# Turning the attended heads on VectorE in an adaLN transformer block on one core

## The chip, the cores and the metric

The kernel runs on one core of one Trainium2 chip. A core has TensorE (matmuls into PSUM), VectorE, ScalarE (ACT), GpSimd (POOL), SyncE (SP, which here only issues DMAs and waits), 16 DMA engines, SBUF with 128 partitions, and PSUM, which the kernel uses as eight buffers of 128 x 512 f32. The metric is the device time of one execution in microseconds (us).

## The reference

One transformer block with adaptive layer norm, batch 1, 2048 rows, width 640, 32 heads of 20 channels, feed-forward width 1536, everything in bfloat16:

```
mod = (silu(c) @ w_mod) -> sa, ca, ga, sb, cb, gb        (six rows of 640)
h = layernorm(x) * (1 + ca) + sa
q, k, v = split(h @ wqkv)                                 (32 heads of 20)
s = q k^T / sqrt(20), kept where 0 <= i - j < 256, else -1e9
x = x + ga * (concat_heads(softmax(s) v) @ wo)
h = layernorm(x) * (1 + cb) + sb
x = x + gb * ((sigmoid(h @ w_gate) * (h @ w_up)) @ w_down)
```

## The kernel before, in words

The 2048 rows are worked in eight chunks of 256 (two blocks of 128 rows). Of each chunk: the layer norm's statistics (VectorE, L781) and a normalized copy `x0`; a turn to channels-on-partitions `hT` (TensorE for chunks 0 and 1, transposing DMAs on SyncE from chunk 2, L810); modulate on VectorE, ACT or POOL (L827, L828); Q, K, V by `wq`, `wk`, `wv` (`qkv`, 5 matmuls of 128x128 by 320 each). Q and K leave PSUM through casts into a staging tile `stg`, each head in 32 columns, and are turned into `QT`, `KT` (TensorE for chunks 0 and 1, DMAs on SyncE after). Scores of one half chunk (16 heads, `q` = 0 or 1) are made transposed, keys on partitions, four heads at a time in row groups of TensorE; ACT takes the exp out of PSUM (L1054, L1028, L1091), POOL masks the window's edges (L1059, L1063, L1032), and `burst` multiplies by V, which carries columns of ones, so that the sums of the softmax come out beside the heads. In chunks from 1 on, the PV matmuls of one half chunk stand in one TensorE block with the scores of the next (`with_pv`).

The attended chunk then stands with 32 channel rows per head (20, and a row of the sum) on partitions and rows of x along the free axis. `norm` turns it in blocks of 32 x 32 on VectorE (`tr1`, L1150, twice per half chunk), takes reciprocals (L1155), multiplies (divide, L1157) into `Tn`, and turns back (`tr2`, L1159) into `On`. `close` writes the 20 used rows of each of four row groups to DRAM (four DMAs on SyncE to `doc`, helper L576), and reads them back into `oT` as channels packed on 128 partitions (one DMA per half chunk). `outproj` multiplies `oT` by `wo`, adds x (L1240), and goes on with the second norm, its turn (`h2T`, DMAs on SyncE, L810) and `mlp`: gate and up by pairs of 128-channel tiles, tanh on ACT (L1285), the product on VectorE (L1287), and `wd`, with the residual add (L1306) and the store. The output of attention and of the MLP is scaled by the gates `ga`, `gb`: instead, `wo` (`wos`, L1331) and `wd` (`wds`, L1268) are multiplied once by the broadcast gate `gbc`, which takes a small trip through DRAM (`gate`, then `gbc`, both on SyncE).

The order of every instruction on every engine is fixed beforehand: the program lists some 2000 operations, and `PLAN` is a permutation of them with an engine for each (`schedule`, L151). The planner follows the list with a model of durations only to hand out buffers; `emit` (L262) writes each engine's stream in that order, with waits on semaphores. So an operation that waits holds up everything behind it in its engine's stream, DMA issues on SyncE included. TensorE's two kinds of blocks, whole-array matmuls (helper line L686) and matmuls in row or column groups (L687: scores, PV, the modulation), alternate in the order given.

Of the kernel before, what the change touches and what calls it, by code (L numbers as in the profile page):

```python
# [8 lines left out]
ALU = mybir.AluOpType  # L9
# [4 lines left out]
D = 640  # L14
H = 32
DH = 20
# [332 lines left out]
def c_pe(n):  # L349
# [118 lines left out]
]  # L468
TR1 = 2
NPH = 2  # L470
NPQ = 2
PQ = ()
# [26 lines left out]
def build(nc, A_x, A_wqkv, A_wo, B_x, B_w_gate, B_w_up, B_w_down, c, w_mod, out, S=2048):  # L499
# [59 lines left out]
    def R(name):  # L559
        return Res(name)  # L560
# [825 lines left out]
```

## Time and profile before

| | us |
|---|---|
| median of 3 runs | 326.38 (326.34 to 329.38) |
| profiled execution | 326.74 |
| its span | 324.8 |
| TensorE busy | 316.1 (97%) |
| ScalarE busy | 213.0 (66%) |
| VectorE busy | 205.6 (63%) |
| GpSimd busy | 188.0 (58%) |
| TensorE idle, 11.3 to 80 us | 2.89 |
| TensorE idle, 80 to 322.2 us | 0.02 |

How to read the rows shown below. A timeline row has the start, the time from the start of the first to the end of the last instruction of the row, the engine and line, the operation, `out<-in`, the shapes and the count, and in brackets the idle time ahead with the engine and line that ended it. "issue" is a wait for nothing that the profile shows. PE is TensorE's matmuls, PEld its weight loads, SPq SyncE's issuing of DMAs. A row of groups has the count, then busy us, mean ns of one, and idle time ahead with its releasers. Matmuls are pipelined and their ends are modelled; starts are what to compare.

### The profile page before, as it was taken

The page shows a single profiled execution, that of the slowest core. Times are in us where ns is not written, and L with a number is a line of the kernel's source. Part 1 is how long each engine was busy: PE and PEld are TensorE (multiplying, and loading weights), DVE is VectorE, ACT ScalarE, POOL GpSimd, SP SyncE. Part 2 cuts the span into 40 slices and gives each one's busy share as a digit, 9 for nine tenths or more (in the row PEclk, how much of TensorE's full clock was granted, in tenths as well). Part 3 has the DMA queues.
Part 4 walks back from the last instruction along what each step waited for, and adds up shares of the span by engine and source line. Part 5 has one row for each costly group of instructions (what it writes and reads, how often), then busy time and mean ns, then how long its engine had stood idle before and what let it go on. Part 6 is the DMA issues. An engine that isn't in the chain of part 4 may idle for free.

```text
span 324.8 us, 11997 instructions
## 1 busy us (share of the span) xinstructions
PE 316.1 (97%) x5044; PEld 236.8 (73%) x5045; DVE 205.6 (63%) x426; ACT 213.0 (66%) x228; POOL 188.0 (58%) x349
## 2 busy tenths in 40 slices
PE   6999999989999999999999999999999999999996
PEld 2666767667776777776787777777888777887885
DVE  4699987768686865674755647464845376645423
ACT  2699984788678877988685857676886756320220
POOL 5337858855868677948774846676583958001000
PEclk9999999999999999999999999999999999999999
DMA  7999989998648464726551303465121206112201
GB/s 238 370 315 245 281 161 189 207 192 281 186 91 140 64 139 75 109 60 130 118 71 26 83 2 73 126 65 120 39 47 28 77 22 83 38 46 41 83 0 42
DMA packets 73023, 38.20 MB, mean 118 GB/s; under 512 B 46602, under 2 KB 71690, under 8 KB 72970
## 3 DMA queue, kind: packets, MB, share of 16 engines
q1 hardware_dynamic: 71808, 36.13, 50.6%
q10 hardware_dynamic: 1162, 1.31, 1.5%
q8 instruction: 40, 0.66, 0.9%
q14 instruction: 13, 0.11, 0.1%
HBM read 21.30 MB, written 5.25 MB: 82 GB/s over the span
## 4 chain that ended last, share of the span: by engine, by line
PE 76%; DVE 0%; issue 0%
PE M L686 64%; PE S L687 6%; PE M L687 5%; DVE x L1306 0%
## 5 line engine op out<-in xcount | busy, mean ns | idle before, releaser
L1054 ACT ACTIVATE E<-S 128x2048 bf16<-128x2048 f32 x56 | 105.0, 1876 | 45.7 <-PE S L687 45.4
L1063 POOL TENSOR_SCALAR_AFFINE_SELECT E<-E 128x512 bf16<-128x512 bf16 x112 | 69.6, 635 | 8.4 <-DVE Tn L1157 2.1
L1059 POOL TENSOR_SCALAR_AFFINE_SELECT E<-E 128x256 bf16<-128x256 bf16 x112 | 45.4, 415 | 48.3 <-PE M L686 14.8
L686 PE MATMUL M<-h2T,wu 128*128 128x256 bf16 x480 | 68.0, 273 | 0.5 <-DVE h2T L828 0.5
L686 PE MATMUL M<-h2T,wg 128*128 128x256 bf16 x480 | 67.0, 273 | 0.0
L686 PE MATMUL M<-wd,hh 128*128 128x320 bf16 (+2 forms) x396 | 57.3, 296 | 0.0
L1287 DVE SCALAR_TENSOR_TENSOR hh<-sig,M 128x512 bf16<-128x512 f32 x48 | 32.2, 680 | 34.9 <-ACT sig L1285 24.1
L686 PEld LDWEIGHTS M<-h2T,wu 128*128 128x128 bf16 x480 | 45.3, 98 | 8.4 <-issue 0.7
L686 PEld LDWEIGHTS M<-h2T,wg 128*128 128x128 bf16 x480 | 45.5, 98 | 6.9 <-DVE T L1150 0.2
L686 PEld LDWEIGHTS M<-wd,hh 128*128 128x128 bf16 x396 | 37.0, 98 | 14.0 <-DVE hh L1287 0.2
L1285 ACT ACTIVATE sig<-M 128x512 f32<-128x512 f32 x48 | 28.2, 596 | 27.7 <-PE M L686 27.1
L1032 POOL TENSOR_SCALAR_AFFINE_SELECT E<-E 128x1024 bf16<-128x1024 bf16 x28 | 31.9, 1144 | 6.8 <-DVE st L781 2.5
L1306 DVE TENSOR_TENSOR x<-M,x 128x320 bf16<-128x320 f32 (+2 forms) x33 | 15.7, 479 | 29.4 <-PE M L686 28.9
L687 PE MATMUL S<-QT,KT 20*64 20x256 bf16 (+5 forms) x1856 | 32.3, 228 | 1.3 <-issue 0.7
L687 PEld LDWEIGHTS S<-QT,KT 20*64 20x64 bf16 (+1 forms) x1856 | 20.0, 100 | 18.4 <-issue 8.8
L781 DVE BATCH_NORM_STATS2 st<-x 128x6 f32<-128x320 bf16 x64 | 28.9, 477 | 1.3 <-DMA x<-in_A_x_dram 1.0
L1150 DVE STREAM_TRANSPOSE T<-M 128x512 f32<-128x512 f32 x32 | 21.4, 698 | 13.1 <-PE S L687 10.5
L1028 ACT ACTIVATE E<-S 128x2048 bf16<-128x2048 f32 x14 | 26.3, 1876 | 5.1 <-PE S L687 5.0
L686 PE MATMUL M<-wq,hT 128*128 128x320 bf16 x160 | 25.9, 300 | 1.5 <-ACT hT L827 0.9
L686 PE MATMUL M<-wv,hT 128*128 128x320 bf16 x160 | 26.8, 300 | 0.0
L686 PE MATMUL M<-wk,hT 128*128 128x320 bf16 x160 | 26.2, 300 | 0.0
L686 PE MATMUL M<-wo,oT 128*128 128x320 bf16 x160 | 24.8, 300 | 0.0
(86 smaller groups left out, 362.7 us busy)
## 6 DMA issues: line engine op xcount, KB each, us to landing
x<-in_A_x_dram SPq DMA_DIRECT2D x19, 160.0 KB, 8.4
doc<-On SPq DMA_DIRECT2D x64, 40.0 KB
out_dram<-x SPq DMA_DIRECT2D x14, 160.0 KB, 1.8
wd<-in_w_mod_dram SPq DMA_DIRECT2D x6, 320.0 KB
wd<-in_B_w_down_dram SPq DMA_DIRECT2D x4, 480.0 KB
wu<-in_w_mod_dram SPq DMA_DIRECT2D x5, 320.0 KB
oT<-doc SPq DMA_DIRECT2D x8, 192.0 KB
wg<-in_B_w_gate_dram SPq DMA_DIRECT2D x2, 576.0 KB
```

What stands on the lines that cost most here:

```text
L686: return e.matmul(o, l, r, start=st, stop=sp, skip_group_check=True)
L687: return e.matmul(o, l, r, start=st, stop=sp, tile_position=tp, skip_group_check=True)
L781: A("dve", lambda e, g, bi=bi, j=j: e.bn_stats(v(bi * 12 + j * 6, 6), src[bi].ap[:, j * 320:(j + 1) * 320]), 0.48, reads=[src[bi].r()], wr ...
L1028: A("act", lambda e, eng: e.activation(cell().rearrange("p m (x c) -> p m x c", c=64)[:, :, 0:4:3, :], Sp.ap[:].rearrange("p j (k x c) -> ...
L1032: A("pool", lambda e, eng, c0=c0, pat=pat, base=base, cm=cm: e.affine_select(cell()[:, :, c0:c0 + 64], cell()[:, :, c0:c0 + 64], pattern=p ...
L1054: A("act", lambda e, eng: e.activation(part(0, 512), Sp.ap[:], ACT.Exp, scale=SM_SCALE), 1.876, reads=[Sp.r()], writes=[E.r("C"), E.r("B") ...
L1059: A("pool", lambda e, eng, hc=hc, src=src, far_h=far_h: e.affine_select(side(hc), part(src, 64), pattern=[[0, 4], [-1 if far_h else 1, 64] ...
L1063: A("pool", lambda e, eng, c0=c0, near=near: e.affine_select(part(c0, 128), part(c0, 128), pattern=[[0, 4], [1 if near else -1, 128]], com ...
L1150: A("dve", lambda e, g, h=h: e.transpose(T1.ap[:, 512 * h:512 * h + 512], X[h].ap), 0.694, reads=[X[h].r()], writes=[T1.r(h)], prio=3.5, t ...
L1285: A("act", lambda e, g, pg=pg, sg=sg: e.activation(sg.ap[:], pg.ap[:], ACT.Tanh, scale=0.5), c_act(512), reads=[pg.r()], writes=[sg.r()], ...
L1287: A("dve", lambda e, g, pu=pu, sg=sg, f0=f0: e.scalar_tensor_tensor(out=hh.ap[:, f0:f0 + 2, :], in0=sg.ap[:].rearrange("p (a b) -> p a b", ...
L1306: A("dve", lambda e, g, ps=ps, bi=bi, c0=c0, n=n: e.tensor_tensor(x1[bi].ap[:, c0:c0 + n], ps.ap[:, 0:n], x1[bi].ap[:, c0:c0 + n], op=ALU. ...
```

## The change

`norm` now divides into a `Tn` of 128 x 1280 that takes both half chunks, ordered so that, after the second half, two turns on VectorE (128 x 640, one per block of 128 rows) write `oT` directly. The tile `On`, the DRAM tensor `doc`, its 64 writes and 16 reads are gone, and with them the clearing of `Tn`. Each block of `oT` is waited for by itself (`oT.r(bi)`), no longer each half of the heads.

For this, heads are numbered `16q + 4j + k` (row group `j`, set `k`) instead of `4(4q + k) + j`; the cast of Q and K into `stg` permutes accordingly. Partition `32j + r` of tile `t` of `oT` now holds channel `32t + r` of the 160 channels of the eight heads of row group `j`, so `wo` is loaded with its rows in that order: sixteen DMAs of 16 partitions by 2 or 3 rows on SyncE, in place of one of 128 partitions by 5 rows. The five `wos` follow, each with its own resource.

`PLAN` is another order, with other engines for some of the casts, modulates and stores. Operations by queue or engine, before and after: SyncE 205 and 133, ACT 236 and 244, VectorE 426 and 424, POOL 337 and 337, TensorE 959 and 959. Two durations in the planner's model differ (0.29 to 0.25 and 0.25 to 0.262). All five `wos` stand on VectorE, in a row.

```diff
-TR1 = 2
...
-    p_Tn = sbpool("Tn", 1, [128, 1024])
-    p_On = sbpool("On", 1, [128, 1024])
+    p_Tn = sbpool("Tn", 1, [128, 1280])
...
+    R_wo = [R(f"wo{t}") for t in range(NDT)]
+    R_wop = {(j, x, q): R(f"wo{j}{x}{q}") for j in range(4) for x in range(2) for q in range(2)}
...
-    for i in range(len(p_Tn.aps)):
-        p_Tn.init[i].append(A("pool", lambda e, g, i=i: e.memset(p_Tn.aps[i][:], 0.0), 1.0, writes=[R("ti")], prio=3))
...
-    dma(lambda: wo[:], lambda: A_wo.rearrange("(t p) f -> p t f", p=128), 2.15, writes=[R_wo], prio=0.5, tag="wo")
+    for j in range(4):
+        for x in range(2):
+            cut = 3 - x
+            for q, t0, t1 in ((0, 0, cut), (1, cut, NDT)):
+                r0 = 80 * j + 16 * x if q == 0 else 320 + 80 * j + 16 * (1 - x)
+                dma(lambda j=j, x=x, t0=t0, t1=t1: wo[32 * j + 16 * x:32 * j + 16 * x + 16, t0:t1, :],
+                    lambda t0=t0, t1=t1, r0=r0: A_wo.rearrange("(u e) f -> e u f", e=16)[:, r0 // 16:r0 // 16 + 2 * (t1 - t0) - 1:2],
+                    0.055 * (t1 - t0), writes=[R_wop[j, x, q]], prio=0.5, tag="wo")
...
-                        h = 4 * (4 * q + k) + j
+                        h = 16 * q + 4 * j + k
...
-    def norm(X, On, a):
-        T1, Tn, Dr = Tile(p_T1, "T1"), Tile(p_Tn, "Tn"), Tile(p_Dr, "Dr")
+    def norm(X, Tn, q, a):
+        T1, Dr = Tile(p_T1, "T1"), Tile(p_Dr, "Dr")
...
-        A("dve", lambda e, g: e.tensor_tensor(blk(Tn), blk(T1), Dr.ap[:].unsqueeze(2).to_broadcast([128, 32, DH]), op=ALU.mult),
-          0.82, port=True, reads=[T1.r(0), T1.r(1), Dr.r()], writes=[Tn.r()], prio=4, tag=f"divide_{a}")
-        A("dve", lambda e, g: e.transpose(On.ap[:], Tn.ap[:]), 1.22, reads=[Tn.r()], writes=[On.r()], prio=4, tag=f"tr2_{a}")
+        A("dve", lambda e, g: e.tensor_tensor(
+            Tn.ap[:].rearrange("p (b k d) -> p k b d", k=8, d=DH)[:, 4 * q:4 * q + 4],
+            T1.ap[:].rearrange("p (k b r) -> p k b r", k=4, r=32)[:, :, :, 0:DH],
+            Dr.ap[:].rearrange("p (k b) -> p k b", k=4).unsqueeze(3).to_broadcast([128, 4, 8, DH]), op=ALU.mult),
+          0.82, port=True, reads=[T1.r(0), T1.r(1), Dr.r()], writes=[Tn.r(q)], prio=4, tag=f"divide_{a}")
...
         def close(q, X):
-            On = Tile(p_On, f"On{a}_{q}")
-            norm(X, On, a)
-            for j in range(4):
-                Rj = R(f"doc{a}_{q}_{j}")
-                dma(lambda j=j, q=q: rdoc[j * DH:(j + 1) * DH, 4 * q:4 * q + 4, :],
-                    lambda j=j, On=On: On.ap[32 * j:32 * j + DH, :].rearrange("p (g c) -> p g c", g=4), 0.22,
-                    reads=[On.r()], writes=[Rj], prio=1, tag=f"n_ow_{a}", dur=0.42)
-                R_doc[q].append(Rj)
-            t0, t1 = ((0, 2), (2, 5))[q]
-            dma(lambda t0=t0, t1=t1: oT.ap[:, t0:t1, :], lambda t0=t0, t1=t1: doc.rearrange("(t p) c -> p t c", p=128)[:, t0:t1, :],
-                0.41, reads=R_doc[0] + (R_doc[1] if q else []), writes=[oT.r(q)], prio=1.5, tag=f"oT_{a}", dur=0.5, dlat=2.88)
+            norm(X, Tn, q, a)
             if q == 1:
+                for bi in range(2):
+                    A("dve", lambda e, g, bi=bi: e.transpose(
+                        oT.ap[:, :, bi * 128:bi * 128 + 128].rearrange("p t (b c) -> p b t c", c=32), Tn.ap[:, 640 * bi:640 * bi + 640]),
+                      0.83, reads=[Tn.r(0), Tn.r(1)], writes=[oT.r(bi)], prio=4, tag=f"tr2_{a}")
                 x1, h2 = outproj(a, oT)
...
-                pe_chain(ps, 320, pairs, [[oT.r(0 if t < 2 else 1), R_wo] for t in range(NDT)], 15, f"wo{a}",
+                pe_chain(ps, 320, pairs, [[oT.r(bi), R_wo[t]] for t in range(NDT)], 15, f"wo{a}",
...
     for t in range(NDT):
         A(WSE[0], lambda e, g, t=t: e.tensor_tensor(wo[:, t, :], wo[:, t, :], gbc[:], op=ALU.mult), WS, port=True,
-          reads=[R_wo, R_gbc], writes=[R_wo], prio=20, tag="wos")
+          reads=[R_wop[j, x, int(t >= 3 - x)] for j in range(4) for x in range(2)] + [R_gbc], writes=[R_wo[t]], prio=20, tag="wos")
```

More of the change, by code (lines that the diff above doesn't have):

```diff
@@ L562, in build @@
     R_w3 = {k: [R(k + "0"), R(k + "1")] for k in ("wq", "wk", "wv")}
-    R_crow, R_ident, R_ccol, R_cth, R_siluc, R_silubc, R_wo = (R(n) for n in ("crow", "ident", "ccol", "cth", "siluc", "silubc", "wo"))
+    R_crow, R_ident, R_ccol, R_cth, R_siluc, R_silubc = (R(n) for n in ("crow", "ident", "ccol", "cth", "siluc", "silubc"))
+    R_wo = [R(f"wo{t}") for t in range(NDT)]
+    R_wop = {(j, x, q): R(f"wo{j}{x}{q}") for j in range(4) for x in range(2) for q in range(2)}
     R_wg = [[R(f"wg{t}_{h}") for t in range(NDT)] for h in range(2)]
@@ L933, in qkv @@
                     if not PAIR:
-                        evac(lambda s=s, half=half: heads(s.ap[:, half * 512:half * 512 + 512], 32)[:, :, 0:DH],
-                             lambda ps=ps: heads(ps.ap[:, 0:320], DH), 320, [ps.r()], [s.r(half)], 6, f"evqk{a}")
+                        evac(lambda s=s, half=half: s.ap[:, half * 512:half * 512 + 512].rearrange(
+                            "p (k j x) -> p j k x", k=4, x=32)[:, :, :, 0:DH],
+                             lambda ps=ps: ps.ap[:, 0:320].rearrange("p (j k d) -> p j k d", j=4, d=DH), 320, [ps.r()], [s.r(half)], 6, f"evqk{a}")
                 if PAIR:
@@ L1025, in sc @@
             return ins
-        last["s"] = [with_pv(f"ends{a}", sc, 0.29, set_reads(a, q), [G, Sp], before, 1)]
+        last["s"] = [with_pv(f"ends{a}", sc, 0.25, set_reads(a, q), [G, Sp], before, 1)]
         cell = lambda: G.ap.rearrange("p (m c) -> p m c", c=256)
@@ L1050, in sc @@
             return ins
-        last["s"] = [with_pv(f"score{a}", sc, 0.25, set_reads(a, q), [E, Sp], before, 3)]
+        last["s"] = [with_pv(f"score{a}", sc, 0.262, set_reads(a, q), [E, Sp], before, 3)]
         part = lambda c0, n: E.ap.rearrange("p (j c) -> p j c", j=4)[:, :, c0:c0 + n]
@@ L1130, in pv @@
                     for j in range(4):
-                        h = 4 * (4 * q + k) + j
+                        h = 16 * q + 4 * j + k
                         ins = mm(e, X[bank].ap[32 * j:32 * j + 32, oc:oc + n * 128], V[2 * a + kb].ap[:, h * VW:h * VW + 32],
@@ L1144, in burst @@
         return a, pv, (6 if a else 3) * 512 / 2400.0 * 1.04 + 0.02, rd, X
-    def norm(X, On, a):
-        T1, Tn, Dr = Tile(p_T1, "T1"), Tile(p_Tn, "Tn"), Tile(p_Dr, "Dr")
-        blk = lambda t: t.ap[:].rearrange("p (b r) -> p b r", r=32)[:, :, 0:DH]
-        for h in range(2) if TR1 == 2 else ():
+    def norm(X, Tn, q, a):
+        T1, Dr = Tile(p_T1, "T1"), Tile(p_Dr, "Dr")
+        for h in range(2):
             A("dve", lambda e, g, h=h: e.transpose(T1.ap[:, 512 * h:512 * h + 512], X[h].ap), 0.694, reads=[X[h].r()],
               writes=[T1.r(h)], prio=3.5, tag=f"tr1_{a}")
-        if TR1 == 1:
-            A("dve", lambda e, g: e.transpose(T1.ap[:], Mall[:, X[0].slot:X[0].slot + 2, :].rearrange("p a c -> p (a c)")), 1.23,
-              reads=[X[0].r(), X[1].r()], writes=[T1.r(0), T1.r(1)], prio=3.5, tag=f"tr1_{a}")
         A("dve", lambda e, g: e.reciprocal(Dr.ap[:], T1.ap[:, DH:1024:32]), 0.35, reads=[T1.r(0), T1.r(1)], writes=[Dr.r()],
           prio=4, tag=f"recip_{a}")
-        A("dve", lambda e, g: e.tensor_tensor(blk(Tn), blk(T1), Dr.ap[:].unsqueeze(2).to_broadcast([128, 32, DH]), op=ALU.mult),
-          0.82, port=True, reads=[T1.r(0), T1.r(1), Dr.r()], writes=[Tn.r()], prio=4, tag=f"divide_{a}")
-        A("dve", lambda e, g: e.transpose(On.ap[:], Tn.ap[:]), 1.22, reads=[Tn.r()], writes=[On.r()], prio=4, tag=f"tr2_{a}")
+        A("dve", lambda e, g: e.tensor_tensor(
[3 more added lines that the diff above has]
+          0.82, port=True, reads=[T1.r(0), T1.r(1), Dr.r()], writes=[Tn.r(q)], prio=4, tag=f"divide_{a}")
     pend = []
@@ L1176, in attention @@
     def attention(a):
-        doc = dram(f"doc{a}", [D, CH])
-        rdoc = doc.rearrange("(g r) c -> r g c", r=4 * DH)
-        R_doc = [[], []]
-        oT = Tile(p_oT, f"oT{a}")
+        oT, Tn = Tile(p_oT, f"oT{a}"), Tile(p_Tn, f"Tn{a}")
         def close(q, X):
-            On = Tile(p_On, f"On{a}_{q}")
-            norm(X, On, a)
-            for j in range(4):
-                Rj = R(f"doc{a}_{q}_{j}")
-                dma(lambda j=j, q=q: rdoc[j * DH:(j + 1) * DH, 4 * q:4 * q + 4, :],
-                    lambda j=j, On=On: On.ap[32 * j:32 * j + DH, :].rearrange("p (g c) -> p g c", g=4), 0.22,
-                    reads=[On.r()], writes=[Rj], prio=1, tag=f"n_ow_{a}", dur=0.42)
-                R_doc[q].append(Rj)
-            t0, t1 = ((0, 2), (2, 5))[q]
-            dma(lambda t0=t0, t1=t1: oT.ap[:, t0:t1, :], lambda t0=t0, t1=t1: doc.rearrange("(t p) c -> p t c", p=128)[:, t0:t1, :],
-                0.41, reads=R_doc[0] + (R_doc[1] if q else []), writes=[oT.r(q)], prio=1.5, tag=f"oT_{a}", dur=0.5, dlat=2.88)
+            norm(X, Tn, q, a)
             if q == 1:
+                for bi in range(2):
+                    A("dve", lambda e, g, bi=bi: e.transpose(
+                        oT.ap[:, :, bi * 128:bi * 128 + 128].rearrange("p t (b c) -> p b t c", c=32), Tn.ap[:, 640 * bi:640 * bi + 640]),
+                      0.83, reads=[Tn.r(0), Tn.r(1)], writes=[oT.r(bi)], prio=4, tag=f"tr2_{a}")
                 x1, h2 = outproj(a, oT)
```

224 rows, old and new, of the table PLAN are left out of this document.

## The prediction

> **What bounds the kernel now.** I read the page first (busy times, the chain that ended last), then TensorE by stage in the table of windows, then TensorE's timeline around each hole.
>
> ```profile
> span 324.8 us, 11997 instructions
> PE 316.1 (97%) x5044; PEld 236.8 (73%) x5045; DVE 205.6 (63%) x426; ACT 213.0 (66%) x228; POOL 188.0 (58%) x349
> PE 76%; DVE 0%; issue 0%
> PE M L686 64%; PE S L687 6%; PE M L687 5%; DVE x L1306 0%
> 0.00:11.30 11.30, 8.14 (x78) 3.98 (x80) 4.99 (x18) 3.50 (x7) 4.83 (x22) 1.00 0.83 273
> 11.30:80.00 68.70, 65.81 (x1113) 46.31 (x1114) 56.90 (x129) 56.41 (x70) 45.30 (x81) 1.00 1.04 244
> 80.00:322.20 242.20, 242.18 (x3856) 186.54 (x3853) 143.37 (x280) 153.13 (x153) 137.88 (x247) 1.00 0.37 75
> 322.20:324.80 2.60, 0.00 (x0) 0.00 (x0) 0.29 (x1) 0.00 (x0) 0.00 (x0) 1.00 0.36 110
> ```
>
> TensorE is busy 97% of the span and the chain that ended last is its matmuls, VectorE holding 0% of it. In the table the columns are the stretch, its length, then PE, PEld, DVE, ACT, POOL, the granted clock (1.00 everywhere) and the DMA share. From 80 us to 322.2 us TensorE has no hole at all: 242.18 of 242.20. All that a new order can win lies in the second row, 68.70 − 65.81 = 2.89 us of idle. The head (11.3 us) and the tail (2.60 us) have the same instructions in both kernels.
>
> The change leaves TensorE's instructions as they are: the same 5045 matmuls in the same number of blocks of whole-array and tiled work, by the two programs side by side. Only their order differs. So the question is which holes of the second stage close, and whether new ones open. The holes, from TensorE's timeline:
>
> ```profile
> 36.54 0.39 PE L686 MATMUL M<-ident,stg 128*128 128x128 bf16 x4
> 37.20 0.43 PE L687 MATMUL S<-QT,KT 20*64 20x256 bf16 x24 [0.27 <-ACT E L1054]
> ...
> 42.62 0.40 PE L687 MATMUL S<-QT,KT 20*64 20x256 bf16 x17
> 43.75 0.23 PE L687 MATMUL S<-QT,KT 20*64 20x64 bf16 x7 [0.72 <-issue]
> 43.92 1.26 PE L686 MATMUL M<-wq,hT 128*128 128x320 bf16 x8
> ...
> 61.52 0.43 PE L687 MATMUL S<-QT,KT 20*64 20x256 bf16 x24
> 61.88 1.26 PE L686 MATMUL M<-wq,hT 128*128 128x320 bf16 x8
> ...
> 64.43 0.43 PE L687 MATMUL S<-QT,KT 20*64 20x256 bf16 x24
> 65.79 0.72 PE L686 MATMUL M<-wq,hT 128*128 128x320 bf16 x4 [0.93 <-ACT hT L827]
> ...
> 73.22 0.43 PE L687 MATMUL S<-QT,KT 20*64 20x256 bf16 x24
> 74.20 0.38 PE L686 MATMUL M<-h2T,wu 128*128 128x256 bf16 x2 [0.55 <-DVE h2T L828]
> ```
>
> A block of 24 score matmuls that nothing disturbs takes 61.88 − 61.52 = 0.36 us from its start to that of the next block. That is the ruler for the others. (a) 65.79 − 64.43 − 0.36 = 1.00 us: Q of chunk 4 waits for hT. (b) 43.92 − 42.62 − 0.36 = 0.94 us: a stop in the middle of a score block, after 17 of 24, that waits for nothing the profile shows. (c) 74.20 − 73.22 − 0.36 = 0.62 us: the first gate/up matmul waits for chunk 0's h2T. (d) 0.27 us at 37.20, a score block that waits for an exp. Together 2.83 us. The idle column gives these four 0.93 + 0.72 + 0.55 + 0.27 = 2.47, so 2.89 − 2.47 = 0.42 us is spread in scraps. Ends of matmuls are modelled, which hides some tenths per wait, so I take 4.0 us as the most that can be had.
>
> **The change part by part.** *Holes (a) and (c)* hang on SyncE's queue.
>
> ```profile
> 56.81 0.56 SPq L576 DMA_DIRECT2D wd<-in_B_w_down_dram  x1
> 57.51 2.55 SPq L810 DMA_TRANSPOSE hT<-x  x2
> ...
> 66.84 2.52 SPq L810 DMA_TRANSPOSE h2T<-x  x2
> ```
>
> The hT transposes of chunk 4 were issued at 57.51, behind one Q turn and a wd load. In the new order they stand ahead of all four Q/K turns of chunk 3 with no wd load before them, while Q of chunk 4 stands at the same TensorE work. One turn (half of the 2.55 row, 1.28 us) and the 0.56 load are 1.8 us, more than the 1.00 us late. For (c) the first wo block comes 3.85 us of matmul time earlier and the first h2T matmul 1.6 us later by the new order, so 4.3 us more lie between, from which the out-projection's own spread and a modulate split over ACT and POOL take some; I keep about 1 us of margin and count both holes as closed: −1.62.
>
> *Hole (b)* stops inside a block whose operands are there.
>
> ```profile
> q8 instruction: 40, 0.66, 0.9%
> ```
>
> Forty instruction packets moved 0.66 MB, 16.5 KB each, so the streams are refilled in such blocks, and the one sizeable "issue" wait fits a refill that came late in a stage whose DMA share is 1.04. The new order moves what stands at that count and what the DMA queues carry then: the 64 doc writes are gone. Bounds: −0.94 (gone), 0 (stays), +0.94 (a second one). I take −0.94, since only one of TensorE's many refills showed. [...]
>
> *Hole (d)*: the distances between a score block and the exp it waits for are longer in the new order, with 11 blocks that have none to spare for 23 before. −0.27. From the scraps I take −0.3 of 0.42. New scraps I put at +0.35, one more of the size of (d).
>
> *The turn itself.* Per half chunk the old chain is two turns out of PSUM, reciprocal, divide, a third turn, four DMA writes to DRAM and one read back. The new one divides into a wider tile, and after the second half two turns of 128x640 write oT.
>
> ```profile
> L1159 DVE STREAM_TRANSPOSE On<-Tn 128x1024 bf16<-128x1024 bf16 x16 | 19.9, 1242 | 0.4
> L743 DVE STREAM_TRANSPOSE mt<-M 128x160 f32<-128x160 f32 x2 | 0.7, 334 | 0.0
> ```
>
> A 640-wide turn lies between 334 ns (160 wide) and 1242 ns (1024 wide); on the straight line through both rows, 0.84 us. VectorE saves 8 × (2 × 1.242 − 2 × 0.84) = 6.4 us, all beside a full TensorE, so worth 0. Where it could cost is chunk 7, whose wo block comes closest behind its last PV:
>
> ```profile
> 277.85 0.72 PE L686 MATMUL M<-wd,hh 128*128 128x320 bf16 x4
> 278.40 1.25 PE L686 MATMUL M<-h2T,wg 128*128 128x256 bf16 x10
> 279.50 1.25 PE L686 MATMUL M<-h2T,wu 128*128 128x256 bf16 x10
> ...
> 277.97 1.31 DVE L1150 STREAM_TRANSPOSE T<-M 128x512 f32<-128x512 f32 x2 [1.79 <-PE M L687]
> 279.71 0.82 DVE L1157 TENSOR_TENSOR Tn<-T,Dr 128x640 bf16<-128x640 f32 x1
> ```
>
> From the end of PV (277.85) to the end of the divide (279.71 + 0.82 = 280.53) is 2.68 us, plus a turn of 0.84 is 3.52. The new order puts 34 gate/up matmuls between, at (279.50 − 278.40) / 10 = 0.110 us, 3.7 us. It fits by 0.2; with the upper bound of 1.24 for the turn it misses by 0.2. Elsewhere 8.5 to 16.3 us lie between. Cost taken: 0, bounds 0 to +0.4.
>
> *The sixteen wo loads* and the gate, on SyncE:
>
> ```profile
> 13.79 0.43 SPq L576 DMA_DIRECT2D wu<-in_w_mod_dram  x1
> 19.19 0.33 SPq L576 DMA_DIRECT2D x<-in_A_x_dram  x1
> 21.51 1.01 SPq L576 DMA_DIRECT2D wd<-in_w_mod_dram  x2
> 25.57 1.30 SPq L810 DMA_TRANSPOSE hT<-x  x1
> 29.02 0.63 SPq L576 DMA_DIRECT2D gate<-grow  x1
> 33.87 0.34 SPq L576 DMA_DIRECT2D gbc<-gate  x1
> 36.07 1.32 SPq L576 DMA_DIRECT2D doc<-On  x3
> 38.87 1.40 POOL L1331 TENSOR_TENSOR wo<-wo,gbc 128x640 bf16<-128x640 bf16 x1
> ```
>
> A narrow issue costs 1.32 / 3 = 0.44 us (20 partitions), a wide one 0.43. The queue rests from 14.22 to 19.19 and from 22.52 to 25.57. Five wo loads stand ahead of the x load of 19.19, in the first rest. Seven (3.1 us) and three wu loads that stood before 14.2 (1.3 us) come behind it: the first hT transposes move from 25.57 to 22.52 + 4.4 = 26.9. Gate and gbc follow about 0.9 us late, gbc near 34.8; wos could start 5.0 us after it as before (38.87 − 33.87), at 39.8. VectorE reaches its five wos, now in a row behind a divide, near 41.5. Cover 1.7 us, cost 0. If the cover is gone, VectorE stands at the first wos, with the casts of Q and K, the LN statistics and chunk 0's two turns queued behind it, and TensorE waits for these.
>
> POOL loses its one wos (1.40 us) and a memset and gets two modulates; ACT issues six stores more; some casts change engines. All this stands beside a TensorE that has work: 0, bounds 0 to +0.4. **Sum:** −1.62 − 0.94 − 0.27 − 0.3 + 0.35 = −2.8. The profiled execution took 326.74 us for its span of 324.8, the median of the three runs is 326.38. 326.74 − 2.8 = 323.9 for a profiled execution, 326.38 − 2.8 = **323.6** by the median.
>
> **The rivals.** *B, the change does not do what it says:* the stops move with the order, or new waits come in their place. For it: VectorE and ACT are each busy for 56 of the stage's 68.7 us, and every margin above is 1 to 2 us. If (b) stays and one wait of the size of (a) opens, 323.6 + 0.94 + 1.00 = 325.5; its range 324.6 to 326.8. Against: both late transposes stand clearly earlier.
>
> *C, slower:* the sixteen loads come late and VectorE blocks at the first wos. It decides from gbc 1.7 us later than I have it, that is 0.15 us more for each of the 11 loads behind the x load, 0.59 us an issue. Sixteen of 128 partitions could move at an eighth of the stage's 244 GB/s or at all of it; at a quarter, 800 KB take 13.1 us for 3.3, 9.8 us more; less the cover of 1.7 and some 2 us at the wo block, about 6 us: 329.6, range 326.8 to 332. For it: DMA is full here (1.04). Against: the 20-partition writes at 36.07 issue at 0.44 us, and the loads are spread over 25 us. [...] No row of before shows a 16-partition load.
>
> *D, nearly all holes close:* 326.38 − 4.0 = 322.4 (322.0 to 322.9).
>
> **How the numbers follow.** The forecast's own range is 322.9 to 324.6 (one of the terms missed), chance 0.45. B 0.30, C 0.12, D 0.13. The range takes the forecast, nearly all of B and D's upper part: 322.3 to 327.0. One per cent, 3.3 us, is about what a measurement of this kernel can tell from no change, so faster means below 323.1, slower above 329.6. Faster: D whole and a part of the forecast, 0.13 + 0.19 = 0.32. Slower: the larger part of C, 0.10. The rest, 0.58, lies within.
>
> **What would show it.** Right: no wait above 0.3 us for hT or h2T before 80 us, no "issue" wait inside a score block, TensorE idle of the second stage near 0.5 to 1 us, the 640-wide turn at 0.78 to 0.9 us, and wo of chunk 7 without a wait. Wrong: VectorE idle ahead of wos with a DMA as releaser, a first hT transpose on SyncE after 28 us, a turn above 1.0 us, or a new stop with "issue" elsewhere.

## The result and the profile after

The changed kernel takes 324.73 us (median of 14 runs, 323.86 to 326.09) against 326.51 us before (14 runs, 325.79 to 331.21): ratio 0.9936, 95% interval 0.9914 to 0.9958, so 1.4 to 2.8 us less. The forecast was 323.6 us, 2.8 us less, in a range of 322.3 to 327.0. The profiled execution took 323.86 us, the shortest of the 14, which matters below: a profile shows one execution.

The head of the changed kernel's page, and then its table of windows (columns as before):

```profile
span 321.8 us, 11856 instructions
PE 315.8 (98%) x5045; PEld 236.9 (74%) x5045; DVE 198.6 (62%) x424; ACT 213.6 (66%) x229; POOL 189.0 (59%) x349
```

```profile
0.00:11.30 11.30, 8.56 (x79) 4.11 (x79) 4.92 (x18) 3.42 (x7) 3.94 (x21) 1.00 0.83 273
11.30:80.00 68.70, 67.81 (x1135) 48.39 (x1135) 56.23 (x131) 58.35 (x73) 48.85 (x89) 1.00 1.09 247
80.00:319.20 239.20, 239.20 (x3833) 184.42 (x3831) 137.09 (x275) 151.83 (x151) 136.18 (x240) 1.00 0.28 53
319.20:321.80 2.60, 0.19 (x4) 0.01 (x1) 0.34 (x2) 0.00 (x0) 0.00 (x0) 1.00 0.25 79
```

TensorE's idle time in the second stage went from 2.89 to 68.70 − 67.81 = 0.89 us. From 80 us on it is still without a hole, though the DMA share there fell from 0.37 to 0.28 and VectorE is busy 7.0 us less over the whole span: that bought nothing, as TensorE waited for neither there. Now TensorE's timeline where the four holes were:

```profile
36.62 0.43 PE L687 MATMUL S<-QT,KT 20*64 20x256 bf16 x24
37.60 0.84 PE L687 MATMUL M<-E,V 128*32 128x256 bf16 x32 [0.56 <-ACT V L902]
...
42.34 0.43 PE L687 MATMUL S<-QT,KT 20*64 20x256 bf16 x24
42.70 1.53 PE L686 MATMUL M<-wk,hT 128*128 128x320 bf16 x10
...
62.67 0.43 PE L687 MATMUL S<-QT,KT 20*64 20x256 bf16 x24
63.03 0.85 PE L686 MATMUL M<-wv,hT 128*128 128x320 bf16 x5
63.72 1.52 PE L686 MATMUL M<-wk,hT 128*128 128x320 bf16 x10
...
71.58 1.79 PE L686 MATMUL M<-wv,hT 128*128 128x320 bf16 x12
73.21 0.38 PE L686 MATMUL M<-h2T,wg 128*128 128x256 bf16 x2
```

The score block at 42.34 takes the quiet 0.36 us; K of chunk 4 (63.72) and the first h2T matmul (73.21) follow their neighbours without a gap. Holes (a), (b) and (c) are gone in this execution, and (d) with them. One new wait of 0.56 us stands at 37.60, where chunk 0's PV waits for a cast of V that ACT did late.

SyncE's timeline behind those holes, and then VectorE's at the gate:

```profile
28.80 2.68 SPq L810 DMA_TRANSPOSE hT<-x  x2
37.02 0.37 SPq L572 DMA_DIRECT2D gbc<-gate  x1
54.18 2.69 SPq L810 DMA_TRANSPOSE hT<-x  x2
64.21 2.60 SPq L810 DMA_TRANSPOSE h2T<-x  x2
```

```profile
41.37 0.82 DVE L1154 TENSOR_TENSOR Tn<-T,Dr 128x640 bf16<-128x640 f32 x1
42.10 2.09 DVE L1321 TENSOR_TENSOR wo<-wo,gbc 128x640 bf16<-128x640 bf16 x5
```

The transposes of chunk 4's hT are issued 3.3 us earlier than before (54.18 for 57.51), those of h2T 2.6 us earlier. The gate is 2.2 us later than I had it (37.02 for 34.8), but the five wos still follow the divide at once. They do so by little: gbc landed at 41.87, 0.2 us ahead of the first of them.

### The profile page after: what moved, and what is told of

Its sections match the earlier page's. It is cut to its first block, busy times and chain, and to the rows that moved or that the text cites. A ratio compares the mean times of both kernels' runs of the same rounds, so it can differ in the third digit from the quotient of the medians.

```text
span 321.8 us, 11856 instructions
## 1 busy us (share of the span) xinstructions
PE 315.8 (98%) x5045; PEld 236.9 (74%) x5045; DVE 198.6 (62%) x424; ACT 213.6 (66%) x229; POOL 189.0 (59%) x349
## 4 chain that ended last, share of the span: by engine, by line
PE 93%; DMA 3%; DVE 1%; ACT 1%; issue 0%; ACTq 0%; DVEq 0%
PE M L686 77%; PE S L687 8%; PE M L687 7%; DMA hT<-x 2%; DMA x<-in_A_x_dram 1%; PE S L686 1%; ACT hT L819 1%; DVE st L781 1%; PE S L678 0%; DVE x L803 0%; ACT stg L902 0%; DVE KT L903 0%; ACTq L572 0%; DVE st L783 0%; ACT hT L902 0%
## 5 line engine op out<-in xcount | busy, mean ns | idle before, releaser
L1060 POOL TENSOR_SCALAR_AFFINE_SELECT E<-E 128x256 bf16<-128x256 bf16 x112 | 46.4, 424 | 57.4 <-ACT E L1055 24.6
L1064 POOL TENSOR_SCALAR_AFFINE_SELECT E<-E 128x512 bf16<-128x512 bf16 x112 | 70.3, 643 | 4.6 <-DVE x L803 1.2
L686 PE MATMUL M<-h2T,wu 128*128 128x256 bf16 x480 | 66.7, 273 | 0.0
L686 PEld LDWEIGHTS M<-wd,hh 128*128 128x128 bf16 x396 | 37.2, 98 | 13.6 <-DVE hh L1277 0.2
L686 PE MATMUL M<-wk,hT 128*128 128x320 bf16 x160 | 27.9, 299 | 0.0
L686 PE MATMUL M<-wv,hT 128*128 128x320 bf16 x160 | 26.1, 299 | 0.0
L686 PE MATMUL M<-wo,oT 128*128 128x320 bf16 x160 | 25.9, 299 | 0.0
```

The source lines that it names most:

```text
L686: return e.matmul(o, l, r, start=st, stop=sp, skip_group_check=True)
L1060: A("pool", lambda e, eng, hc=hc, src=src, far_h=far_h: e.affine_select(side(hc), part(src, 64), pattern=[[0, 4], [-1 if far_h else 1, 64] ...
L1064: A("pool", lambda e, eng, c0=c0, near=near: e.affine_select(part(c0, 128), part(c0, 128), pattern=[[0, 4], [1 if near else -1, 128]], com ...
```

## The experiments

**The changed kernel again.** No edit. Two more profiles, in two sessions, because the first was of the shortest execution.

> The changed kernel as it is, to see what its profile shows when it takes the usual 324.7 us instead of the 323.86 us of its first profile. Theory refill: a stop with issue as releaser, 0.7 to 1.0 us, in the middle of a block near 42 or 54 us, where TensorE's instruction refills came latest; TensorE idle from 11.3 to 80 us then 1.7 to 1.9 us for 0.89. Theory gate: gbc lands later than 41.5 us, VectorE stands ahead of its five wos (L1321), and TensorE waits up to 0.9 us for a cast or for oT behind them. If the profiled execution takes 323.9 again, both leave it as it was.

> The changed kernel once more, beside the three below on the same chip: 324.3 to 325.3 us. Theory refill: where its profile takes 324.4 us or more, the sixth refill lands less than 1.3 us before TensorE reaches the end of its block near 57 us, and an issue stop stands there.

Measured: 324.97 us (12 runs), ratio to before 0.9947 (0.9921 to 0.9974), profiled execution 324.40; then 324.37 us (6 runs), ratio 0.9905 (0.9874 to 0.9937), profiled 323.64. TensorE's timeline of the first, and VectorE's at the gate:

```profile
56.64 0.40 PE L687 MATMUL S<-QT,KT 20*128 20x64 bf16 x30
57.74 0.20 PE L687 MATMUL S<-QT,KT 20*128 20x64 bf16 x2 [0.70 <-issue]
```

```profile
41.69 0.81 DVE L1154 TENSOR_TENSOR Tn<-T,Dr 128x640 bf16<-128x640 f32 x1
42.66 2.10 DVE L1321 TENSOR_TENSOR wo<-wo,gbc 128x640 bf16<-128x640 bf16 x5 [0.16 <-DMA gbc<-gate]
```

The stop inside a score block is back, at another place and 14 us later than in the kernel before. The gate theory does not explain it: VectorE waited ahead of wos in this one of the three profiles, for 0.16 us, and no wait of TensorE stands behind it before the stop at 57.74.

The stop is not what makes this execution 0.5 us longer than the first one either. TensorE's first Q matmul starts at 11.76 us for 11.40, so 0.36 us of it was lost in the head; from there to the end of the span it is 310.6 us for 310.4, as the wait for V at 37.6 us is not there this time.

**Bulk loads later, in the kernel before.** The edit, in SyncE's order:

```
 x<-in_A_x_dram x2
-doc<-On
-wg<-in_B_w_gate_dram 128x3x768
-doc<-On x3
-wu<-in_B_w_up_dram 128x3x768
+doc<-On x4
 hT<-x x2
 ...
 KT<-stg x2
+wg<-in_B_w_gate_dram 128x3x768
+wu<-in_B_w_up_dram 128x3x768
 QT<-stg
```

> The kernel before with two weight loads of 576 KB (wg at 35.63, wu at 37.43 us) issued only behind the KT transposes near 54 us; nothing else moved. Theory refill (the issue stop of 0.94 us near 43 us is an instruction refill that queued behind these loads): the refill packet that started at 41.36 us starts near 38 us, the stop goes, TensorE reaches its later blocks about 0.9 us earlier; time 0.4 to 0.9 us less, as the hole at 65 us may take some back. Theory other: the stop stays at 0.6 to 1.0 us, ratio 0.998 to 1.002.

Measured: 330.38 us, ratio 1.0114 (1.0071 to 1.0158). The stop near 43 us is gone, as the refill theory says, but it is gone without this edit too in one profile (*wd_behind*, below), so its absence here does not show that the loads made it. The time is 3.4 us more:

```profile
42.59 0.43 PE L687 MATMUL S<-QT,KT 20*64 20x256 bf16 x24
42.95 1.53 PE L686 MATMUL M<-wq,hT 128*128 128x320 bf16 x10
...
68.76 1.25 PE L686 MATMUL M<-wq,hT 128*128 128x320 bf16 x4 [4.87 <-ACT hT L827]
```

The two loads now stand ahead of chunk 4's hT transposes, and the hole at 65 us grew from 1.0 to 4.9 us. The windows behind it show a second cost, in the column of the granted clock:

```profile
65.00:70.00 5.00, 1.24 (x5) 0.73 (x6) 1.06 (x3) 2.39 (x5) 1.20 (x2) 0.73 1.24 223
70.00:75.00 5.00, 5.00 (x45) 2.72 (x43) 1.47 (x3) 2.16 (x3) 2.95 (x7) 0.59 1.13 186
```

From the hole on the granted clock is 0.50 until 74.1 us, so for some 5 us of TensorE's work.

What makes the stop can be put in numbers. The trace's packets of the instruction queue give the start and landing of each refill. Forty refills for the 10,188 recorded instructions of TensorE are some 256 each, and the stops stand at the same two counts in every profile, 1216 to 1217 and 1728 to 1729, two times 256 apart, so I take them for the points where the instructions of a refill begin. All profiles that show such a stop, and two that show none at the old place, worked out from these records ("left" is the time from the landing to the start of the last matmul ahead of that point, "step" from there to the start of the next one; 0.11 is a step with nothing in it):

```
run            refill starts  lands   last matmul ahead      left   step to the next
before            41.36       42.43        42.84             0.41        0.91
path_alone        42.28       43.38        42.78            -0.59        2.02
wd_and_pool       41.85       42.78        42.77            -0.01        1.44
wd_behind         39.58       40.52        42.64             2.12        0.11
bulk_later        39.05       40.76        42.73             1.97        0.11
bulk_away         39.74       40.78        41.88             1.10        0.30
one_wo_load       39.78       40.73        41.69             0.95        0.39
after             54.84       55.81        56.94             1.13        0.27
again             55.45       56.46        56.85             0.39        0.89
again2            54.55       55.55        56.64             1.09        0.34
bulk_away         55.26       56.21        56.57             0.36        0.86
trip_chunk7       55.08       56.04        56.43             0.39        1.08
ends_later        55.24       56.20        57.11             0.91        0.50
```

The two last columns add up to 1.2 to 1.5 us wherever TensorE stopped: by these rows a refill was of use some 1.3 us after its packet had landed, and TensorE stopped for what was missing of that. What makes a packet start late is not shown. The kernels *before*, *wd_behind* and *wd_and_pool* have the same order up to 52 us and issue the two loads at nearly the same times, and their refill started at 41.36, 39.58 and 41.85: so hole (b) comes and goes from one execution to the next. The start of 39.05 without the loads ahead of it is earlier than all three, but its packet took 1.7 us and landed no earlier than that of *wd_behind*.

**The new turn in the old order.** No DRAM trip, one wo load, and otherwise the old order of instructions. The edit is the diff of the change without its `PLAN`, with

```diff
+    dma(lambda: wo[:], lambda: A_wo.rearrange("(t p) f -> p t f", p=128), 2.15, writes=list(R_wop.values()), prio=0.5, tag="wo")
```

for the sixteen loads; the first half's `tr2` is dropped, and both new turns stand at the second's place.

> The new turn (no DRAM trip, two turns of 640) and the new head order, in the old order of instructions, with wo as one load of 128 partitions (its rows are not permuted, so the output is another one). Theory order (the gain comes from where instructions stand, the shorter path is worth nothing by itself): ratio to the kernel before 0.998 to 1.002, holes of about 1.0 us at 65 us, 0.6 us at 74 us and the issue stop near 43 us still there. Theory path (64 writes and 16 reads fewer in the DMA queues and on SyncE bring the gain): 0.993 to 0.996, holes at 65 and 74 us closed.

Measured: 330.45 us, ratio 1.0117 (1.0076 to 1.0157). Neither theory: it is slower.

```profile
42.56 0.40 PE L679 MATMUL S<-QT,KT 20*64 20x256 bf16 x17
44.80 0.23 PE L679 MATMUL S<-QT,KT 20*64 20x64 bf16 x7 [1.83 <-issue]
...
65.48 0.43 PE L679 MATMUL S<-QT,KT 20*64 20x256 bf16 x24
68.42 1.20 PE L678 MATMUL M<-wq,hT 128*128 128x320 bf16 x4 [2.51 <-ACT hT L819]
```

Without the doc writes between them, the two bulk loads of 576 KB are issued earlier (35.09 and 35.56 us for 35.63 and 37.43), the refill starts at 42.28 for 41.36, and the stop doubles; that the one makes the other is not shown. The second hT transpose of chunk 4 is issued 1.3 us later than before (60.10 for 58.83) and lands 2.6 us later (67.25 for 64.62), so the second hole grows from 0.93 to 2.51 us of idle, and the granted clock behind it is 0.50 for 3.4 us (68.5 to 71.9). So the shorter path alone, in an order made for the longer one, costs 1.2%; the gain comes only with the order.

**One wo load.** The changed kernel with the line above for its sixteen loads, at the place of the eighth.

> The changed kernel with wo as one load of 128 partitions at the place of the eighth of the sixteen (rows not permuted, so the output is another one). Theory loads cost nothing (as forecast): ratio to before 0.992 to 0.996, as the changed kernel. Theory loads cost (15 issues of 0.44 us on SyncE put the gate 2 us later than forecast): gbc is issued near 33 to 34 us for 37.0, the wait of 0.56 us at 37.6 us goes, and the median falls by 0.5 to 1.4 us to 323.3 to 324.2.

Measured: 323.74 us (8 runs), ratio 0.9915 (0.9879 to 0.9950), beside 324.97 us of the changed kernel on the same chip. The intervals overlap; some 1 us is the best estimate of what the sixteen loads cost. The profiles show less of it: from the first Q matmul to the end of the span it is 310.0 us here, and 310.2 to 310.6 in the three profiles of the changed kernel. SyncE and TensorE:

```profile
22.48 1.14 SPq L571 DMA_DIRECT2D wd<-in_w_mod_dram  x1
28.55 2.69 SPq L802 DMA_TRANSPOSE hT<-x  x2
36.24 0.34 SPq L571 DMA_DIRECT2D gbc<-gate  x1
```

```profile
27.56 0.84 PE L678 MATMUL M<-wv,hT 128*128 128x320 bf16 x5
...
36.37 0.43 PE L679 MATMUL S<-QT,KT 20*64 20x256 bf16 x24
36.72 0.84 PE L679 MATMUL M<-E,V 128*32 128x256 bf16 x32
```

SyncE is through with its loads at 23.6 us and issues the first hT transposes at 28.55 all the same, for 28.80. Their rows are there (VectorE ended the first block at 24.95). What they wait for is a buffer: `hT` has two, and chunk 2 takes that of chunk 0, whose last V matmul, the last of the row at 27.56, ends at 28.40. So the sixteen issues do not hold them. The gate gains 0.8 us, which nothing uses. TensorE reaches chunk 0's PV at 36.72 for 37.60, without the wait for V.

**wo in eight loads**, four of 128 partitions and four of 32, alone and together with the edit of *The score block later* below:

```diff
+    halves = [A_wo[320 * n:320 * n + 320, :].rearrange("(j c) f -> j c f", j=4) for n in range(2)]
+    for t, n, c0 in ((0, 0, 0), (1, 0, 32), (3, 1, 16), (4, 1, 48)):
+        dma(lambda t=t: wo[:, t, :], lambda n=n, c0=c0: halves[n][:, c0:c0 + 32, :], 0.44, writes=[R_wol[t]], prio=0.5, tag="wo")
+    for j in range(4):
+        dma(lambda j=j: wo[32 * j:32 * j + 32, 2, :], lambda j=j: A_wo.rearrange("(g r) f -> g r f", r=16)[5 * j + 4:5 * j + 21:16], 0.11,
+            writes=[R_wo2[j]], prio=0.5, tag="wo")
```

> The changed kernel with wo, its rows in the right order, in eight loads: four of 128 partitions and four of 32, at the places of eight of the sixteen. Theory loads cost: SyncE issues 8 loads fewer (3.5 us), the first hT transposes stand before 27.5 us for 28.8, gbc near 34.5 for 37.0, median 0.5 to 1.2 us below the changed kernel's, as with one load (323.74). Rival (only the change of moment counted): within 0.3 us of the changed kernel.

> Both edits, eight loads and the score block later. If both theories hold: 323.0 to 323.6 us and no issue stop before 80 us; if only the loads count, as wo_in_eight.

Measured: 328.09 us, ratio 1.0008 (0.9983 to 1.0033), and 328.80 us, ratio 1.0051 (1.0023 to 1.0078); the changed kernel beside them 324.37. A miss, by 4 us and the wrong way. TensorE in the first:

```profile
28.45 0.40 PE L685 MATMUL S<-QT,KT 20*128 20x256 bf16 x8
31.00 1.26 PE L685 MATMUL M<-wu,silubc 128*32 128x160 bf16 x40 [2.15 <-DMA wu<-in_w_mod_dram]
```

The modulation's weights land too late: three wide wo loads stand ahead of the last of them on SyncE, where the one load stood behind all of them. TensorE loses 2.2 us and then runs at a granted clock of 0.50 from 31.3 to 34.7 us, an estimated 1.7 us more; later it waits 0.9 us for V and 0.6 us for an exp. Why seven narrow loads ahead of the same weights do less harm is open.

**Transposes ahead of the wd loads, in the kernel before.** SyncE's order:

```
 QT<-stg
+hT<-x x2
 wd<-in_B_w_down_dram
-hT<-x x2
 ...
 QT<-stg
+h2T<-x x2
 wd<-in_B_w_down_dram
-h2T<-x x2
```

and a second kernel in which, besides, two of POOL's masks go behind the normalization of chunk 4.

> The kernel before with two wd loads (480 KB each, issued at 56.81 and 66.04 us) moved behind the transposes of hT (57.51) and h2T (66.84); nothing else moved. Theory queue (as forecast: both transposes stand behind loads on SyncE and in the DMA queues): the hole at 65 us falls from 1.0 to below 0.3 us, that at 74 us from 0.6 to below 0.2, time 1.0 to 1.5 us less than before. Rival data (the hT transposes wait for POOL, which ends the normalized rows at 57.44 us): the hole at 65 us stays between 0.7 and 1.1 us, that at 74 us shrinks by 0.4, time 0.3 to 0.6 us less.

> As wd_behind, and two of POOL's masks (1.2 us, at 52.8) behind the normalization of chunk 4, whose hT transposes then stand ahead of the wd load. Theory queue: no more than wd_behind gives, within 0.2 us. Rival data: the transposes are issued 0.7 us earlier than 57.51, the hole at 65 us falls to 0.3 us or less, time 0.6 to 0.9 us below that of wd_behind.

Measured: 328.2 us, ratio 1.0049 (1.0018 to 1.0079), and 329.96 us, ratio 1.0114 (1.0073 to 1.0155): both slower. Of the first, TensorE and VectorE:

```profile
42.49 0.43 PE L687 MATMUL S<-QT,KT 20*64 20x256 bf16 x24
42.85 1.53 PE L686 MATMUL M<-wq,hT 128*128 128x320 bf16 x10
...
65.49 1.11 PE L686 MATMUL M<-wk,hT 128*128 128x320 bf16 x7 [0.82 <-DVE x L803]
...
74.56 0.38 PE L686 MATMUL M<-h2T,wu 128*128 128x256 bf16 x2 [1.77 <-DVE h2T L828]
```

```profile
73.27 0.89 DVE L1268 TENSOR_TENSOR wd<-wd,gbc 128x640 bf16<-128x640 bf16 x2 [2.24 <-DMA wd<-in_B_w_down_dram]
74.08 0.60 DVE L828 TENSOR_SCALAR h2T<-h2T,scB,shB 128x256 bf16<-128x256 bf16 x2
```

The score block of hole (b) runs through in this execution (42.49 to 42.85), though the edit moves nothing before 56 us. Q of chunk 4 no longer waits for hT. POOL's and SyncE's rows of this run, and POOL's of the kernel before, show why:

```profile
54.65 1.72 POOL L800 TENSOR_SCALAR x<-x,st 128x640 bf16<-128x640 bf16 x2
55.57 2.54 SPq L810 DMA_TRANSPOSE hT<-x  x2
```

```profile
55.72 1.72 POOL L800 TENSOR_SCALAR x<-x,st 128x640 bf16<-128x640 bf16 x2
```

Each of the two transposes needs one of POOL's two blocks of rows. Here the first is issued as soon as the first block is ready (55.52 us); in the kernel before the block was ready at 56.59 and the transpose was issued at 57.51, right behind the wd load. And the transposes land sooner: 2.7 and 2.6 us after their issue (at 58.25 and 59.49), for 3.7 and 5.8 us (at 61.20 and 64.62) with the load ahead of them. Those of h2T land at 70.52 for 73.47. So the queue theory had the mechanism right for both, and the time wrong.

The time goes to what comes next. K stands 0.82 us; the row names VectorE, but TensorE waits there for a KT transpose of chunk 3 too, which lands at 65.36 us, as in the kernel before (65.27), where hole (a) hid it. And VectorE now waits 2.24 us for the wd load that was moved back, with the modulate of h2T queued behind it: the hole at 74 us grows from 0.55 to 1.77 us, and the granted clock behind it is 0.50 for 3.4 us (75.4 to 78.8). In the second kernel the hT transposes again land 2.6 to 2.7 us after their issue, and TensorE waits for the masks that were moved back:

```profile
58.25 2.11 PE L687 MATMUL M<-E,V 128*32 128x256 bf16 x48 [2.58 <-POOL E L1063]
```

so its time does not tell the two theories apart.

**One wd load away, in the changed kernel**, to let the sixth refill start earlier: `wd` of 47.52 us behind the bulk loads at 71 us, and two of the `wds` down VectorE's order behind it.

> The changed kernel with the first wd load (480 KB, issued at 47.52 us) moved behind the bulk loads near 71 us, and the two wd multiplications that need it moved down VectorE to the others at 86 us. Theory refill: the sixth refill of TensorE's instructions, which started at 54.84 us (no stop) and 55.45 us (stop of 0.89 us) in the two profiles of the changed kernel, starts near 53 us and never stops TensorE; median 0.4 to 0.9 us below the changed kernel's, about 324.1, and its executions closer together. Rival: the spread comes from the gate or from V and ACT, median within 0.3 us of the changed kernel's.

Measured: 338.12 us, ratio 1.0379 (1.0335 to 1.0423). TensorE waits 12.3 us for a POOL mask (L1064) near 87 us; POOL waits by the planner's rule for the VectorE multiplication ahead of it, and that for the load. The edit broke another thing, so its time tells nothing of the refill. Its profile tells a little: the refill started at 55.26, within the 54.55 to 55.45 of the three profiles with the load in place, and the stop stood there. So that load alone does not decide it.

**The score block later.** TensorE's order in the changed kernel:

```
-wk,hT x5
-S<-QT,KT 128x64 x32
-wk,hT x7
+wk,hT x10
+S<-QT,KT 128x64 x32
+wk,hT x2
```

> The changed kernel with one score block of 32 (near 56.6 us, in which the block of instructions ended in the profiles with a stop) moved behind the next five wk matmuls. Theory refill: TensorE reaches the end of that block some 0.6 us later, the stop of 0.7 to 0.9 us shrinks to 0.2 or less, median 0.3 to 0.7 us below the changed kernel's. Rival (the spread comes from elsewhere, or the exp behind the block, 0.7 us later, makes TensorE wait instead): within 0.2 us of it, or above.

Measured: 324.59 us (12 runs), ratio 0.9920 (0.9896 to 0.9945), beside 324.37. No gain.

```profile
57.61 0.24 PE L687 MATMUL S<-QT,KT 20*128 20x64 bf16 x7 [0.31 <-issue]
...
59.83 0.43 PE L687 MATMUL S<-QT,KT 20*64 20x256 bf16 x24 [0.51 <-ACT E L1029]
```

The stop is 0.31 us, for 0.70 in *again* and 0.15 in *again2*, so this one profile does not show that the edit shrank it; the refill theory had 0.2 or less. The exp behind the block, now late, made TensorE wait 0.51 us, as the rival says.

**The DRAM trip back, for chunk 7 alone.**

```diff
+            if a == NCH - 1:
+                On = Tile(p_On, f"On{a}_{q}")
+                A("dve", lambda e, g: e.transpose(On.ap[:], Tn.ap[:, 0:1024]), 1.22, reads=[Tn.r(0)], writes=[On.r()], prio=4, tag=f"tr2_{a}")
...
```

with the four writes and the read of the old `close`.

> The changed kernel with the old way through DRAM for the last chunk alone (a turn of 1024, four writes and a read per half; the heads land in another row order than wo, so that chunk's output is another one). Theory: the new order needs the short chain; in the old kernel the read of oT was issued 6.8 us after the end of PV and lands some 2 to 2.9 us later, 9 to 9.7 us against 3.7 us of matmuls between, so TensorE waits 5.3 to 6.0 us ahead of wo of chunk 7 and the time is 5 to 6.5 us above the changed kernel's, 330 to 331. Rival (the DRAM trip is hidden anyway): within 1 us of 324.8.

Measured: 332.9 us, ratio 1.0212 (1.0167 to 1.0257).

```profile
285.96 0.38 PE L687 MATMUL M<-h2T,wu 128*128 128x256 bf16 x2
291.87 2.83 PE L687 MATMUL M<-wo,oT 128*128 128x320 bf16 x10 [5.53 <-issue]
```

TensorE waits 5.5 us, as forecast for the longer chain. ("issue" here: the row does not see that it is the landing of the second read of oT, at 291.78 us by the trace.) The span is another 1.9 us longer: the granted clock is 0.50 for some 3 us behind the hole (to 294.6 us), and a refill stop of 0.9 us stands near 56 us. So the new order can only stand on the short chain.

## Why the prediction was right or wrong

**What bounds it, and the sum.** Right in the main: of the 3.0 us of the first profile, 2.0 are idle time of TensorE in the second stage. The rest the forecast had as unchanged: by the windows 0.6 are idle time in the head and the tail, and 0.3 are busy time (316.1 and 315.8). In the three profiles of the changed kernel the span is 3.0, 2.5 and 3.2 us shorter, for the 2.8 forecast; over the runs of the first session it is 1.4 to 2.8, by the ratios of the two later ones about 1.7 and 3.1. The profiles flatter the change a little, as the three profiled executions are the first or second shortest of their sessions. The median of 324.73 lies inside the stated range and 0.1 us above the forecast's own, 322.9 to 324.6, in that of rival B. That the sum came so near is partly luck, by these and by hole (b).

**Holes (a) and (c)** closed, −1.62 as costed, and the step named was the right one: the wd load ahead of the transposes on SyncE held them, by 0.9 us at the issue of the first and by some 3 us at the landing of the second (wd_behind). What the forecast did not have is the rest. POOL has the first block of rows ready 2.4 us earlier in the new order (54.16 for 56.59), and hT lands at 59.47 for 64.62. And with the loads alone moved, the next waits came up at once, for KT and behind VectorE's wait for the wd load: the closing of the two holes needed the new order as a whole.

**Hole (b)** was a refill that came late: every stop stands at one of two counts of instructions, two refills apart, and ends 1.2 to 1.5 us behind a landing. The step that failed is its size, "I take −0.94, since only one of TensorE's many refills showed". The stop is not a fixture of the order: in three profiles of the old order up to there the step was 0.91, 0.11 and 1.44 us. The new order has its own tight place, the sixth refill, with steps of 0.27, 0.89 and 0.34 us. The means are 0.82 and 0.50 us, so an estimate from these few profiles is that 0.3 us of the 0.94 is won. The bound "0 (stays)" should have had weight for executions, not only for kernels. Why the median lies 0.9 us above the first profile is open: the first two profiles differ by 0.36 us in the head alone, and no execution above 324.40 us was profiled. In each profile at least 38 of some 40 refills show no stop of TensorE; the stops seen at the others were of 0.2 to 1.8 us.

**Hole (d) and new scraps.** The wait for exp went; a wait of 0.56 us for V came within a microsecond of its place (0.3 us in the third profile). With one of 0.15 us at 13.6 us, the new waits of the first profile are twice the +0.35 forecast for them.

**The turn.** One row of groups of the changed kernel, and chunk 7:

```profile
L1182 DVE STREAM_TRANSPOSE oT<-Tn 128x640 bf16<-128x640 bf16 x16 | 13.3, 837 | 0.2
```

```profile
282.15 0.83 PE L686 MATMUL M<-h2T,wg 128*128 128x256 bf16 x6
...
285.87 1.52 PE L686 MATMUL M<-wo,oT 128*128 128x320 bf16 x10
```

```profile
284.86 1.57 DVE L1182 STREAM_TRANSPOSE oT<-Tn 128x640 bf16<-128x640 bf16 x2
```

837 ns for the 0.84 us of the straight line. From PV's end (282.15) to the end of the first turn (284.86 + 0.84 = 285.70) are 3.55 us, to the first wo matmul 3.72: the forecast's 3.52 and 3.7, and it fits by the 0.2 us forecast.

**The sixteen loads.** Cost 0, and that was mis-sized: about 1 us by one_wo_load, of which its profile shows 0.2 to 0.6. Not for the reason I worked through. The queue of issues ended at 27.87 us for the 26.9 forecast, and no one waited for it: the first hT transposes came at 28.80, held by the buffer that chunk 0's V matmuls still read, and at 28.55 without the loads. The cover at wos was 0.2 us and not 1.7, and once it was missed by 0.16. What the profiles show of the cost is the wait for V at 37 us, which is there in two of the three profiles of the changed kernel (0.56 and 0.29 us) and not with one load.

**The rivals.** B came true in part, by the refill. C came close and cost nothing: gbc was issued 2.2 us later than I had it, past the 1.7 at which C decides, but VectorE reached wos at 42.1 for 41.5, and stood there in one profile only, for 0.16 us. What share of the rate 16 partitions reach, the quarter that C takes, no run shows: the 60 KB loads of 16 partitions landed in 5.9 us at the median, the 320 KB loads of 128 partitions around them in 4.5 to 5.5.

**The signs.** Three signs of being wrong came while the time stayed in the range. "A first hT transpose after 28 us" is a sign whose mechanism I had misread, as it waits for TensorE's V matmuls. "A new stop with issue elsewhere" is there in two of the three profiles, and "VectorE idle ahead of wos with a DMA as releaser" in one.

## What to carry to other kernels

When one engine is full, a shorter path is worth what its order can make of it: here the path alone cost 1.2% and the order with it won 0.6%, and the single moves that closed a hole (bulk_later, wd_behind) opened the next. Ask of each transfer that is moved which landing it stands ahead of, instruction refills included: TensorE's instructions came here in some 40 packets, each with a due time, and every stop stood in a block of short matmuls (24 in 0.36 us, against 1.53 us for ten of 128x320), where that time comes soonest. Take more than one profile before reading a microsecond out of one: the stop that gave hole (b) its price was absent in another execution of the same order.

## What the runs showed of the hardware that was not expected

A hole of about 2 us on TensorE cost more than itself here. After idle steps (from the start of one matmul to that of the next) of 1.96 to 2.9 us in five of these kernels (path_alone, wd_behind, wd_and_pool, wo_in_eight and wo_in_eight_ends) the granted clock fell to 0.50 for 3.4 us (path_alone 68.5 to 71.9 us, wd_behind 75.4 to 78.8), by which some 1.7 us more are lost, an estimate. After 5.06 us (bulk_later) it was at 0.50 for 6.8 us, which began within the hole, and after 5.80 us (trip_chunk7) for 3.4. Steps of 0.9 to 1.9 us left it at 1.00, and so did one of 2.02 us (path_alone, at 44.80), so these runs give no sharp bound. In wd_behind the clock fell 0.8 us after TensorE had gone on (75.4 for 74.56). And TensorE's refills, 16,384 bytes each, took 0.9 to 2.0 us for the packet (before, after), and where TensorE stood waiting its instructions ran 1.2 to 1.5 us after the landing. Chunk 4's transposing DMAs, issued right behind a 480 KB load, landed 3.7 to 7.2 us after their issue (before, path_alone), and 2.6 to 2.7 us with that load moved behind them (wd_behind, wd_and_pool); in the changed kernel, without that load but among others, it was 4.0 to 4.8.
